# The sum across partitions in a spectral filter: two VectorE instructions, or two accumulating DMAs from GpSimd

## The chip, the cores and the metric

The kernel runs on one core of a Trainium2 chip. The metric is the device time of one execution in microseconds (us), as a median of several runs. The engines are TensorE (PE in the profile; its weight loads are PEld), VectorE (DVE), ScalarE (ACT), GpSimd (POOL) and SyncE (SP), which here only issues DMAs. Each has a queue of its own and takes its instructions in order. SBUF is the memory on the chip, with 128 partitions; matmuls write to PSUM. SP, ACT and GpSimd can issue DMAs.

## The reference

A spectral filter over the sequence, then a block with a low-rank mixing of the sequence and an MLP over the channels:

```python
# x: (8, 3136, 256); filt_r, filt_i: (1569, 256)
X = np.fft.rfft(x, axis=1)
Y = X * (filt_r + 1j * filt_i)[None]
y = np.fft.irfft(Y, n=3136, axis=1)

h = y.transpose(0, 2, 1) @ U @ V                 # U: (3136, 32), V: (32, 3136)
u = y + h.transpose(0, 2, 1)
out = u + np.maximum(u @ w_ch1, 0.0) @ w_ch2     # 256 -> 1024 -> 256
```

Inputs and outputs are float32; inside, the kernel works in float16 with sums in float32.

## The kernel before, in words

The 3136 points are split as 49 x 64, and both transforms are done by matmuls. For each of the 8 batches:

- `f1` (L206, evictions L211) transforms over the 49 points. Frequencies k1 = 1 to 24 with real and imaginary part, and k1 = 0, go to DRAM (`ct1`, `ct0`). For batches 0 and 1 `f1_turned` and `turn` (L231, L256) do the same without the way through DRAM.
- `mid` takes the frequencies in 13 pairs (`PAIRS`; k1 = 0 stands alone as the third). For each: a matmul over the 64 points (`pz`, L318; L320 for k1 = 0), with 64 real parts on partitions 0 to 63 and 64 imaginary parts on partitions 64 to 127; one VectorE product with the real and the imaginary part of the filter at once (L326), which leaves two products `uv[:, 0]` and `uv[:, 1]`; and stage 3 (`s3`: matmul `pe`, L287, eviction by ScalarE to `e3`, L296; L290 for k1 = 0). A tile `uv` holds two pairs (k1 = 0 has one of its own), three such tiles are in rotation, and `s3` runs three pairs behind.
- A complex product needs sums across the halves: the real half takes away the imaginary half's second product, the imaginary half adds the real one's. In batches 1 to 7 L330 and L331 do this on VectorE when a tile is complete, in place, so `s3` needs one matmul. In batch 0 it is left to PE: a second matmul with the weights `gsm`, which are `gm` with its halves swapped and a sign.
- `s3` stores its results to DRAM (`ct2`, L301), and `load_e2` (L343) reads them back into `eb` with k1 on partitions 32 to 79. The row of k1 = 0 goes the same way: one store (L291), and four loads `load_e20` into partition 80 (L346). `eb` has one buffer.
- `rank` (L353 to L364) makes the low-rank term in the frequency domain from `e3` and puts it into partitions 0 to 31 of `eb` with VectorE (L364). `s4` (L379, evictions L384, L386) transforms back over k1 into `ut`.
- The MLP runs in 49 groups of 512 points, each of 8 steps: `mm1` (L411) with ReLU on ScalarE (L414), and for the group before `mm2` (L434) with the residual (L426), an eviction by VectorE every fourth step (L441) and a store every eighth (L446).

`x` is loaded from GpSimd's queue (L110), as it is cast to float16 on the way; so are the filters (L137, L139), whose copies to partitions 64 to 127 `spread_filters` makes (L144, L145). Nearly all other DMAs are issued by SP.

The order: all that comes before `first.close()` (batch 0, and half of `f1` for batch 1) is issued as written. From there, the MLP's 392 steps are the backbone. A section is the 48 steps of one batch's MLP; `deal` spreads the next batch's `mid` over the section's steps 2 to 24 (8 to 31 in the first section), then its `eb` loads, `rank` and `s4`; `f1` of the batch after it is spread from step 18 (28 in the first) on, and the loads of `x` at steps 4, 9, 14 and 19. What is written in this way is a priority: a scheduler sets the order on each engine ahead of the run, and lets an instruction go ahead of its place when it reckons that its inputs are there. In the trace the loads of the k1 = 0 row are issued from 139.62 us on, before the last stores L301 of the same `mid`, which are written ahead of them.

Of the kernel before, what the change touches and what calls it, by code (L numbers as in the profile page):

```python
# [25 lines left out]
def _consts():  # L26
    f16 = np.float16
    q, r = np.arange(NQ), np.arange(NR)
    k2 = np.concatenate([np.arange(32), np.arange(63, 31, -1)])
    k1 = np.arange(1, NK)  # L30


    ws = np.zeros((98, 32, 98))
    for h in range(2):
        for j in range(32):
            w = np.exp(-2j * np.pi * np.outer(64 * q + 32 * h + j, k1) / SEQ)
            ws[h::2, j, 24 * h:24 * h + 24] = w.real
            ws[h::2, j, 48 + 24 * h:72 + 24 * h] = w.imag
            ws[h::2, j, 96 + h] = 0.5

    e = np.exp(-2j * np.pi * np.outer(r, k2) / NR) / 8
    a2 = np.block([[e.real, e.imag], [-e.imag, e.real]])
    a2[:, 96:] *= -1
    f = e.T
    g = np.block([[f.real, -f.imag], [f.imag, f.real]])
    g[96:] *= -1
    gs = np.roll(g, 64, axis=0)
    gs[64:] *= -1  # L50

    rows = [64 * c + 32 * h + j for j in range(32) for c in range(2) for h in range(2)]
    m64 = np.concatenate([a2[rows], g, gs, 2 * a2], axis=1)


    sv = np.zeros((49, NR, NQ))
    ph = 2 * np.pi * np.outer(k1, np.arange(SEQ)) / SEQ
    ph = ph.reshape(24, NQ, NR).transpose(0, 2, 1)
    sv[0:48:2] = 2 / 49 * np.cos(ph)
    sv[1:48:2] = -2 / 49 * np.sin(ph)  # L60
    sv[48] = 1 / 49

    kr = np.tile(np.eye(RANK), (4, 4))
    return (ws.reshape(98, 32 * 98).astype(f16), m64.astype(f16),
            sv.reshape(49, SEQ).astype(f16), kr.astype(f16))
# [3 lines left out]
def kernel(  # L69
# [19 lines left out]

    ct1 = [nc.dram_tensor(f"ct1_{b}", (32, 96, DM), F16, kind="Internal") for b in range(NB)]  # L90
    ct0 = [nc.dram_tensor(f"ct0_{b}", (NR, DM), F16, kind="Internal") for b in range(NB)]
    ct2 = [nc.dram_tensor(f"ct2_{b}", (49, NR, DM), F16, kind="Internal") for b in range(NB)]

    cst = ctx.enter_context(tc.tile_pool(name="cst", bufs=1))
    sb = ctx.enter_context(tc.tile_pool(name="sb", bufs=1))
# [46 lines left out]
    def spread_filters(i):  # L142
        s = slice(PARTS[i], PARTS[i + 1])
        nc.vector.tensor_copy(fab[64:128, 0, s, :], fab[0:64, 0, s, :])  # L144
        (nc.scalar.copy if i else nc.vector.tensor_copy)(fab[64:128, 1, s, :], fab[0:64, 1, s, :])  # L145

    for i in range(3):
        load_filters(i)
# [117 lines left out]
    def mid(b, tag="z"):  # L266
# [14 lines left out]
        def s3(ks, uv, o):  # L281
            n = len(ks) * DM
            i = (ks[0] - 1) // 2
            m = 128 if ks[0] else 64
            pe = ps.tile([128, 512], F32, tag=tag, bufs=2, name="pe")
            for f, w in enumerate((gm, gsm) if b == 0 else (gm,)):
                nc.tensor.matmul(pe[0:m, 0:n], w[:, 0:m], uv[:, f, o:o + n], start=(f == 0), stop=(b > 0 or f == 1))  # L287
            if not ks[0]:
                e3[b, 6] = sb.tile([64, DM], F16, tag="e30", bufs=2, name="e30")
                nc.scalar.copy(e3[b, 6], pe[0:64, 0:n])  # L290
                nc.sync.dma_start(dram(ct2[b], 48 * NR * DM, [[DM, 64], [1, DM]]), e3[b, 6])  # L291
                return
            if i % 2 == 0:
                e3[b, i // 2] = sb.tile([128, 4, DM], F16, tag="e3", bufs=7, name="e3")
            t = e3[b, i // 2]
            nc.scalar.copy(t[:, 2 * (i % 2):2 * (i % 2) + 2, :].rearrange("p k d -> p (k d)"), pe)  # L296
            if b == 0 and i > 9:
                nc.sync.dma_start(dram(ct2[b], 2 * i * 128 * DM, [[DM, 128], [128 * DM, 2], [1, DM]]),
                                  t[:, 2 * (i % 2):2 * (i % 2) + 2, :])
            elif i % 2:  # L300
                nc.sync.dma_start(dram(ct2[b], 2 * (i - 1) * 128 * DM, [[DM, 128], [128 * DM, 4], [1, DM]]), t)  # L301
# [6 lines left out]
        for i, ks in enumerate(PAIRS):  # L308
            n = len(ks) * DM
            if b == 0 and i in (2, 6):  # L310
                spread_filters(i // 4 + 1)
            if b < 2 and i in (3, 7):
                load_a2(i // 4 + 1)
            pz = ps.tile([128, 512], F32, tag="z", bufs=2, name="pz")
            if ks[0]:
                src = a2[(ks[0] - 1) // 8]
                k = (ks[0] - 1) % 8
                nc.tensor.matmul(pz, a2m, src[:, k:k + 2, :].rearrange("p k d -> p (k d)"), start=True, stop=True)  # L318
            else:
                nc.tensor.matmul(pz[:, 0:n], a20m, a2[3], start=True, stop=True)  # L320
            o = 512 if ks[0] % 4 == 3 else 0
            if o == 0:
                uv = sb.tile([128, 2, 1024], F16, tag="uv", bufs=3, name="uv")
            zin = bass.AP(tensor=pz.tensor, offset=pz.offset, ap=[[pz.ap[0][0], 128], [0, 2], [1, n]])
            fin = view(fab[:, 0, ks[0], 0:1], 0, [[NK * DM, 2], [1, n]])
            nc.vector.tensor_mul(uv[:, :, o:o + n], zin, fin)  # L326
            todo.append((ks, uv, o))
            if b and (o or not ks[0]):

                nc.vector.tensor_sub(uv[0:64, 0, 0:o + n], uv[0:64, 0, 0:o + n], uv[64:128, 1, 0:o + n])  # L330
                nc.vector.tensor_add(uv[64:128, 0, 0:o + n], uv[64:128, 0, 0:o + n], uv[0:64, 1, 0:o + n])  # L331
            if len(todo) > (3 if b else 2):
                s3(*todo.pop(0))
            yield
        for it in todo:
# [5 lines left out]

    def load_e2(b, g):
        nc.sync.dma_start(eb[32:80, 8 * g:8 * g + 8, :], dram(ct2[b], 8 * g * DM, [[NR * DM, 48], [1, 8 * DM]]))  # L343

    def load_e20(b, g, eng):
        eng.dma_start(eb[80:81, 16 * g:16 * g + 16, :],  # L346
                      dram(ct2[b], (48 * NR + 16 * g) * DM, [[NR * DM, 1], [1, 16 * DM]]))

    def rank(b):
        ph = ps.tile([128, 512], F32, tag="z", bufs=2, name="ph")  # L350
# [127 lines left out]
    next(ranks[0])  # L478
    for g in range(8):
        load_e2(0, g)  # L480
        if g % 2 == 0:
            load_e20(0, g // 2, nc.scalar)
    for _ in ranks[0]:
        pass

# [16 lines left out]

    def loads(b):
        for g in range(8):
            if g % 2 == 0:
                load_e20(b, g // 2, nc.sync)
            load_e2(b, g)
        yield

    for b in range(1, NB):  # L510
        a, z = S[b - 1], S[b]
        e = z - 17 if b == 1 else z - 24
        deal(mids[b], 17, a + {1: 8, 2: 5}.get(b, 2), e)
        plan[e + 2].append(loads(b))
        deal(ranks[b], 5, e + 3, e + 8)
        deal(s4s[b], 16, e + 8, z)
        if b == 1:
            deal(f1s[1], 4, 0, 6)
        if b + 1 < NB:
            for c in range(4):  # L520
                plan[a + (1 if b == 1 else 4) + (2 if b == 1 else 5) * c].append(later_x(b + 1, c))
            deal(f1s[b + 1], 8, a + (28 if b == 1 else 18), z - (6 if b == 1 else 13))
# [40 lines left out]
```

## Time and profile before

| | |
|---|---|
| median of 3 runs (lowest to highest) | 559.17 us (558.14 to 560.31) |
| the profiled execution | 556.45 us |
| its span, first to last instruction | 554.7 us |
| busy: PE, DVE, ACT, POOL | 519.0, 388.6, 344.3, 37.1 us |
| L326, 96 products of 128 x 1024 / 8 of 128 x 512 | 113.5 / 5.4 us, 1219 / 681 ns each |
| L330 and L331, 42 each of 64 x 1024 | 28.9 and 28.8 us, 687 and 685 ns each |
| L330 and L331, 7 each of 64 x 256 | 2.0 and 2.0 us, 288 and 285 ns each |
| L441, 98 evictions of the MLP | 66.6 us, 684 ns each |
| DMA packets, MB, mean rate | 86174, 88.43 MB, 159 GB/s |
| of these from GpSimd's queue | 7632 packets, 15.94 MB |
| SP issues of `eb` by L346 (k1 = 0) | 28 of 8 KB, median 317 ns each |

The times are of one profiled execution; it is shorter than the median of the runs by 2.7 us. "Busy" of PE is modelled, since matmuls overlap, so a high share does not say that PE runs at its peak; the number of matmuls in a stretch of time says more. A row of a group names the line, the engine, the operation and the tiles, with the number of instructions, their busy time, and the mean of one. The DMA share is a mean over the 16 DMA engines.

### The profile page before, as it was taken

To read this page: it belongs to the slowest core of one execution; us is meant where nothing else is said; L and a number is where in the kernel's file an instruction comes from. 1 tells how busy PE (TensorE), PEld (TensorE's weight loads), DVE (VectorE), ACT (ScalarE), POOL (GpSimd) and SP (SyncE) were. 2 spreads that over 40 slices of the span, in tenths; PEclk is the share of its full clock that TensorE was granted. 3 is DMA by queue.
4 is the path that set the end of the run, shared out by engine and by line. 5 is a ranking of instruction groups with operands and counts; after the bars stand their busy time and mean duration, and the time that the engine had idled before them with its cause. 6 is when DMAs were issued, how large, how long until landed. Compare 5 with 4: busy or idle time off the path is not lost.

```text
span 554.7 us, 11907 instructions
## 1 busy us (share of the span) xinstructions
PE 519.0 (94%) x4794; PEld 353.0 (64%) x4794; DVE 388.6 (70%) x542; ACT 344.3 (62%) x629; POOL 37.1 (7%) x61
## 2 busy tenths in 40 slices
PE   4766999999999899999999999999999999999997
PEld 4425656776667656676567856676667755676665
DVE  3975598777996399776997489775987489751111
ACT  3766777646775557645775557646675567656663
POOL 6541000100010000000010000000000000000000
PEclk9985899999999999999999999999999999999999
DMA  9997624983579635865499454874458334622113
GB/s 192 170 231 177 115 80 118 255 244 135 124 175 290 182 101 129 231 180 193 105 216 291 104 176 118 224 198 155 128 162 250 109 108 134 189 81 77 53 63 113
DMA packets 86174, 88.43 MB, mean 159 GB/s; under 512 B 5059, under 2 KB 76803, under 8 KB 86088
## 3 DMA queue, kind: packets, MB, share of 16 engines
q1 hardware_dynamic: 78480, 71.72, 41.7%
q0 software_dynamic: 7632, 15.94, 17.0%
q8 instruction: 37, 0.61, 0.4%
q14 instruction: 17, 0.14, 0.1%
q10 hardware_dynamic: 8, 0.03, 0.0%
HBM read 55.43 MB, written 48.17 MB: 187 GB/s over the span
## 4 chain that ended last, share of the span: by engine, by line
PE 65%; DVE 14%; DMA 8%; issue 4%; ACT 2%; SPq 1%; POOL 1%; ACTq 0%; POOLq 0%
PE phh L411 24%; PE pc L434 23%; DVE uv L326 7%; PE pu L379 5%; DMA eb<-ct 3%; PE pz L318 3%; PE pe L287 3%; PE pc L426 3%; DMA a<-ct 3%; PE pf L206 3%; DVE uv L330 2%; DVE uv L331 2%; DVE och L441 2%; ACT h L414 1%; POOL sv L170 1%
## 5 line engine op out<-in xcount | busy, mean ns | idle before, releaser
L414 ACT ACTIVATE h<-phh 128x512 f16<-128x512 f32 x392 | 232.6, 598 | 154.7 <-PE phh L411 149.7
L434 PE MATMUL pc<-w2sb,h 128*128 128x256 f16 x1568 | 246.0, 272 | 0.0
L411 PE MATMUL phh<-ut,w1sb 128*128 128x512 f16 (+7 forms) x896 | 241.3, 354 | 1.8 <-ACT h L414 1.2
L434 PEld LDWEIGHTS <-h 128*128 128x128 f16 x1568 | 148.7, 97 | 87.8 <-issue 8.0
L326 DVE TENSOR_TENSOR uv<-pz,fab 128x1024 f16<-128x1024 f32 (+1 forms) x104 | 118.3, 1177 | 11.9 <-PE pz L318 10.5
L441 DVE COPY och<-pc 128x512 f32<-128x512 f32 x98 | 66.6, 684 | 84.2 <-PE pc L426 84.1
L411 PEld LDWEIGHTS <-w1sb 128*128 128x128 f16 x896 | 76.6, 98 | 23.9 <-issue 10.1
L386 DVE CAST ut<-pu 128x392 f16<-128x392 f32 x120 | 65.0, 562 | 33.2 <-PE pu L379 26.9
L296 ACT CAST e<-pe 128x512 f16<-128x512 f32 x96 | 55.4, 587 | 14.3 <-PE pe L287 13.5
L426 PE MATMUL pc<-idn,ut 128*128 128x128 f16 (+1 forms) x400 | 55.3, 219 | 0.0
L379 PEld LDWEIGHTS <-eb 81*128 81x128 f16 x1024 | 42.0, 99 | 11.5 <-issue 3.4
L379 PE MATMUL pu<-sv,eb 81*128 81x49 f16 x1024 | 45.7, 189 | 3.0 <-DMA eb<-ct 2.9
L287 PE MATMUL pe<-uv,m 128*128 128x512 f16 (+1 forms) x117 | 41.4, 384 | 4.0 <-ACT e L296 1.5
L364 DVE COPY eb<-h 32x4096 f16<-32x4096 f16 x32 | 37.7, 1208 | 6.8 <-ACT h L361 6.7
L426 PEld LDWEIGHTS <-ut 128*128 128x128 f16 (+1 forms) x400 | 37.7, 98 | 7.1 <-issue 0.8
L318 PE MATMUL pz<-a,m 128*128 128x512 f16 x96 | 35.8, 385 | 5.8 <-DMA a<-ct 2.8
L110 POOL DMA_DIRECT2D x<-in_x_dram x36 | 20.9, 584 | 299.4 <-PE pf L206 194.8
L211 DVE CAST asb<-pf 98x512 f16<-98x512 f32 x48 | 32.5, 683 | 8.1 <-PE pf L206 7.9
L206 PE MATMUL pf<-x,ws 98*98 98x256 f16 x192 | 34.7, 273 | 0.4 <-ACT asb L211 0.2
L211 ACT CAST asb<-pf 98x512 f16<-98x512 f32 x48 | 28.3, 589 | 6.9 <-PE pf L206 6.5
L330 DVE TENSOR_TENSOR uv<-uv 64x1024 f16<-64x1024 f16 (+1 forms) x49 | 30.9, 630 | 1.3
L331 DVE TENSOR_TENSOR uv<-uv 64x1024 f16<-64x1024 f16 (+1 forms) x49 | 30.8, 628 | 0.9
(59 smaller groups left out, 183.3 us busy)
## 6 DMA issues: line engine op xcount, KB each, us to landing
out_dram<-och SPq DMA_DIRECT2D x48, 512.0 KB
eb<-ct SPq DMA_DIRECT2D x64, 192.0 KB
ct<-e SPq DMA_DIRECT2D x47, 256.0 KB
x<-in_x_dram POOLq DMA_DIRECT2D x28, 392.0 KB, 7.0
ct<-asb SPq DMA_DIRECT2D x24, 384.0 KB
a<-ct SPq DMA_DIRECT2D x18, 512.0 KB
x<-in_x_dram POOLq DMA_DIRECT2D x4, 384.0 KB, 7.9
ws<-ws SPq DMA_DIRECT2D x1, 600.2 KB
```

The lines of the kernel that those rows point to most:

```text
L211: (nc.vector.tensor_copy if i else nc.scalar.copy)(dst, src)
L287: nc.tensor.matmul(pe[0:m, 0:n], w[:, 0:m], uv[:, f, o:o + n], start=(f == 0), stop=(b > 0 or f == 1))
L296: nc.scalar.copy(t[:, 2 * (i % 2):2 * (i % 2) + 2, :].rearrange("p k d -> p (k d)"), pe)
L318: nc.tensor.matmul(pz, a2m, src[:, k:k + 2, :].rearrange("p k d -> p (k d)"), start=True, stop=True)
L326: nc.vector.tensor_mul(uv[:, :, o:o + n], zin, fin)
L379: last = nc.tensor.matmul(pu[:, NQ * i:NQ * i + NQ], eb[:, 8 * g + i, d], sv[:, 8 * g + i, :], start=(i == 0), stop=True, skip_group_check ...
L386: nc.vector.tensor_copy(dst, src)
L411: nc.tensor.matmul(ph[:, o:o + n], w1sb[:, dh, 128 * t:128 * t + 128], utv(b)[:, dh, t0:t0 + n], start=(dh == 0), stop=(dh == 1), skip_gro ...
L414: nc.scalar.activation(h, ph, RELU)
L426: nc.tensor.matmul(d, w, idn, start=False, stop=(dh == 1), skip_group_check=True)
L434: nc.tensor.matmul(o, gr.h[tt][:, 128 * i:128 * i + 128], w2sb[:, tt, :], start=(tt == 0), stop=False, skip_group_check=True)
L441: nc.vector.tensor_copy(gr.och[:, i - 1:i + 1, :], gr.pc.rearrange("p (j d) -> p j d", d=DM))
```

## The change

VectorE's subtraction and addition (L330, L331) go. In their place GpSimd issues two DMAs per tile `uv`, each of which adds 64 partitions of `uv[:, 1]` to the other 64 partitions of `uv[:, 0]` within SBUF. As these only add, the sign moves into the filter: the copy of its imaginary part on partitions 64 to 127 is made with a factor of -1, and `gs` loses its sign for batch 0. `s3` runs five pairs behind instead of three in batches 1 to 7, `uv` has four buffers instead of three, and `mid` is dealt in 19 pieces instead of 17. The row of k1 = 0 no longer goes through DRAM: one DMA from SP writes it from the 64 partitions of `e3[b, 6]` into partition 80 of `eb`; `load_e20` and the row 48 of `ct2` go.

```diff
-    gs[64:] *= -1
...
-    ct2 = [nc.dram_tensor(f"ct2_{b}", (49, NR, DM), F16, kind="Internal") for b in range(NB)]
+    ct2 = [nc.dram_tensor(f"ct2_{b}", (48, NR, DM), F16, kind="Internal") for b in range(NB)]
...
     def spread_filters(i):
         s = slice(PARTS[i], PARTS[i + 1])
         nc.vector.tensor_copy(fab[64:128, 0, s, :], fab[0:64, 0, s, :])
-        (nc.scalar.copy if i else nc.vector.tensor_copy)(fab[64:128, 1, s, :], fab[0:64, 1, s, :])
+        (nc.scalar.mul if i else nc.vector.tensor_scalar_mul)(fab[64:128, 1, s, :], fab[0:64, 1, s, :], -1.0)
...
                 nc.scalar.copy(e3[b, 6], pe[0:64, 0:n])
-                nc.sync.dma_start(dram(ct2[b], 48 * NR * DM, [[DM, 64], [1, DM]]), e3[b, 6])
+                nc.sync.dma_start(eb[80:81, :, :], e3[b, 6])
                 return
...
             if o == 0:
-                uv = sb.tile([128, 2, 1024], F16, tag="uv", bufs=3, name="uv")
+                uv = sb.tile([128, 2, 1024], F16, tag="uv", bufs=4, name="uv")
...
             if b and (o or not ks[0]):
-                nc.vector.tensor_sub(uv[0:64, 0, 0:o + n], uv[0:64, 0, 0:o + n], uv[64:128, 1, 0:o + n])
-                nc.vector.tensor_add(uv[64:128, 0, 0:o + n], uv[64:128, 0, 0:o + n], uv[0:64, 1, 0:o + n])
-            if len(todo) > (3 if b else 2):
+                for p in range(2):
+                    nc.gpsimd.dma_start(uv[64 * p:64 * p + 64, 0, 0:o + n], uv[64 - 64 * p:128 - 64 * p, 1, 0:o + n],
+                                        accum_op=mybir.AluOpType.add)
+            if len(todo) > (5 if b else 2):
                 s3(*todo.pop(0))
...
-    def load_e20(b, g, eng):
-        eng.dma_start(eb[80:81, 16 * g:16 * g + 16, :],
-                      dram(ct2[b], (48 * NR + 16 * g) * DM, [[NR * DM, 1], [1, 16 * DM]]))
...
     for g in range(8):
         load_e2(0, g)
-        if g % 2 == 0:
-            load_e20(0, g // 2, nc.scalar)
...
     def loads(b):
         for g in range(8):
-            if g % 2 == 0:
-                load_e20(b, g // 2, nc.sync)
             load_e2(b, g)
         yield
...
-        deal(mids[b], 17, a + {1: 8, 2: 5}.get(b, 2), e)
+        deal(mids[b], 19, a + {1: 8, 2: 5}.get(b, 2), e)
```

## The prediction

> **What bounds the kernel now.** I read the page's table of 40 slices first: TensorE (PE) stands at 9 tenths from slice 8 on, and VectorE (DVE) at 7 to 9 in bursts that come back every 64 us. PE "busy" is modelled, so I then asked for busy times in stretches cut at those bursts, where the counts of instructions tell more than the shares. A burst holds one batch's `mid` (its 13 multiplications with the filter); the stretch behind it holds that batch's `eb` loads, `rank` and `s4`.
>
> ```profile
> core 0: us, PE busy (x) PEld busy (x) DVE busy (x) ACT busy (x) POOL busy (x), PEclk, DMA share, GB/s
> 64.00:94.00 30.00, 29.25 (x210) 17.85 (x209) 28.68 (x36) 21.71 (x38) 0.00 (x0) 1.00 0.29 87
> 94.00:128.00 34.00, 33.76 (x390) 24.89 (x389) 21.63 (x34) 20.54 (x38) 2.61 (x4) 1.00 0.91 248
> 128.00:157.50 29.50, 29.05 (x207) 17.30 (x205) 28.15 (x36) 20.89 (x39) 1.11 (x2) 1.00 0.37 98
> ...
> 445.00:474.00 29.00, 28.54 (x191) 16.66 (x192) 26.87 (x33) 19.39 (x35) 0.00 (x0) 1.00 0.34 109
> ```
>
> In the bursts (rows 1, 3, 4) DVE is busy 28.15 of 29.5 us, PE gets through 207 matmuls; in the stretch between (row 2) 390 in 34 us, with DVE at 21.6 of 34. The DMA engines are lightly loaded in the bursts (0.29 to 0.37) and nearly full behind them (0.91). VectorE's timeline in one burst shows the cycle:
>
> ```profile
> 142.04 0.68 DVE L331 TENSOR_TENSOR uv<-uv 64x1024 f16<-64x1024 f16 x1
> 142.75 2.35 DVE L326 TENSOR_TENSOR uv<-pz,fab 128x1024 f16<-128x1024 f32 x2
> 145.03 0.68 DVE L211 CAST asb<-pf 98x512 f16<-98x512 f32 x1
> 145.74 0.69 DVE L330 TENSOR_TENSOR uv<-uv 64x1024 f16<-64x1024 f16 x1
> 146.44 0.68 DVE L331 TENSOR_TENSOR uv<-uv 64x1024 f16<-64x1024 f16 x1
> 147.15 2.35 DVE L326 TENSOR_TENSOR uv<-pz,fab 128x1024 f16<-128x1024 f32 x2
> ```
>
> Two products, one eviction, the exchange (L330, L331), without a gap: 4.4 us for two pairs of k1, of which the exchange is 1.4. Thus in the bursts DVE sets the pace.
>
> PE's need in a burst comes from the chain of waits (start, us, what), which holds only the part of each matmul that nothing overlaps:
>
> ```profile
> 203.48 0.43 PE phh L411 x2
> 203.91 0.22 PE pz L318
> 204.13 0.44 PE pc L434 x4
> ...
> 208.55 0.11 PE pc L426 x2
> ```
>
> Two L411 take 0.43 us, four L434 0.44 and one L426 0.055, together 0.925 for a step of the MLP; one L318 or L287 takes 0.22, and one L206 0.11. The burst 128 to 157.5 has 79 L434 (19.75 steps, 18.3 us), 12 + 13 of L318 and L287 (5.5), 18 of L206 (2.0): 25.8 us of 29.5. By the same counts the seven bursts (64 to 94, 128 to 157.5, 194 to 223, 257 to 285, 320 to 349, 385 to 413, 445 to 474; with 2 us of L256 in the first) need 27, 25.8, 26.2, 24.5, 25.5, 24.2 and 26.3, in all 179.5 us of 202.5. **The most that a free DVE can give is 23 us.** The stretches between need what they last (94 to 128: 27.5 steps 25.4, 28 of L206 3.1, `s4` 5.3, `rank` 1: 34.8 of 34) and give nothing.
>
> **The change part by part.**
>
> *Removed from DVE:* 42 + 42 exchanges of 0.69 us and 7 + 7 of 0.29 (L330 28.9 + 2.0, L331 28.8 + 2.0 us), 61.7 us, 8.8 per burst. DVE's need in a burst falls from about 28 to 19 us, below PE's 25.6 (179.5 / 7). So PE bounds the burst next: 28.9 becomes 25.6 at best.
>
> *Added on GpSimd:* 7 tiles per batch times 2 accumulating DMAs, 98 in all; 84 of 128 KB, 14 of 32 KB. Issue: the x loads show 0.55 us each, 7.7 us per batch on a queue that is busy 37.1 of 554.7 us. The descriptors queue with the x loads. What decides is the wait: stage 3 (L287) reads `uv` now after a DMA has landed. No row shows a transfer from SBUF to SBUF or one that adds. Nearest:
>
> ```profile
> q0 software_dynamic: 7632, 15.94, 17.0%
> ...
> x<-in_x_dram POOLq DMA_DIRECT2D x28, 392.0 KB, 7.0
> ...
> fab<-in_filt_r_dram POOLq DMA_DIRECT2D x2, 128.0 KB, 4.2
> ```
>
> GpSimd's packets take 0.170 x 554.7 x 16 / 7632 = 0.198 us. An x load has 98 rows of 4 KB in SBUF, some 196 packets, 12.25 per engine: 2.4 us. Its landing is 5.2 at least and 7.3 in the median over all loads of that line, so 2.8 to 4.9 is fixed. One accumulation has 64 rows of 2 KB, 4 packets per engine: 0.8 us, or 1.6 if the second read doubles it. So 3.6 to 6.5 us; I take 4.2, the row of the same 128 KB.
>
> The loop: from pz (0.38) by the product (1.22), the first issue (0.55), the second's landing (4.2), three handoffs and half an eviction ahead on DVE (together 0.65) L = 7.0 us. Stage 3 lies now 5 pairs behind, so between the pz that completes a tile and the first L287 on it there are 4 pairs; a burst has 13, thus 4 x 25.6 / 13 = 7.9 us at PE's pace. **7.0 fits in 7.9**, so the body costs nothing. Without that cover a burst lasts 13 x L / 4 = 3.25 L. At the end of a batch cover is thinner: the last product is dealt at step 15 of the section, its L287 at step 20, 5 steps of 0.925 and four L287, 5.5 us; 1.5 us late. PE's order is set ahead of the run and may put MLP matmuls in between, so I count half, 0.75 x 7 = 5 us. At most it is all, 10.5.
>
> *GpSimd's queue in front:* an accumulation waits in order for DVE; behind it stand later x loads, needed tens of us later by `f1`, so they cost nothing. The other way, an x load may stand ahead of an accumulation: 2.4 us of packets, and the wait for its buffer. The page has about one x load per burst (146.24, 216.76, 273.42, 342.77); with 0.9 us to spare 1.5 is left, half of the time: 0.75 x 7 = 5 us. From nothing, if x moves out of the bursts, to twice that.
>
> *A rule against the change:* the x issues take 0.55 us, but 0.95, 0.93 and 1.03 at 105.25, 160.39 and 286.87, each beside an `eb` copy (L364) on DVE. The Trainium skill says in "SBUF — State Buffer", on the two-port modes of DVE, that GpSimd can't write descriptors while such a copy runs; the trace agrees with 0.4 us more. In a burst there is no L364, so at 0.55 the sum stays; with 0.95 for both issues L is 7.8 and still fits.
> The Trainium skill gives in "DMA: Bandwidth & Descriptors", on the anatomy of one DMA, about 2.0 us plus bytes over 436 GB/s, an estimate of 2.3 us here; the sum would then be the full 23 us. The landings above (4.2 and 7.0) speak against so little, though they are from HBM.
>
> *The k1 = 0 row:* one SP DMA from `e30` in place of a store and four loads. 28 SP issues of 0.32 us go (L346), 1.3 us per batch in the bursts, where SP mostly waits for ACT (165 us). Its reader `s4` comes over 20 us after the copy, longer than an `eb` load takes (6.9 in the chain); cost nothing, gain up to the 5.1 us that PE waits for `eb`. I take 0. In batch 0 four ACT issues go (39.81 to 44.87, behind which ACT L237 and PE wait), but `s4` needs `eb` loads that SP issues from 41.98, and the x load that PE waits for at 54.2 is issued at 49.0 behind an `eb` group that lands at 48.5: gain 0 to 3.5, I take 0. The filter's sign in `spread_filters` is one operation for another of 0.48 to 2.75 us: 0, at most 0.5 more. The fourth `uv` buffer and the 19 steps add no instruction.
>
> Sum: -23 + 5 + 5 = **-13 us**. The profiled execution took 556.45 (span 554.7), so 543.4; the median of the three runs is 559.17, 2.7 higher, and the forecast on that scale is **546**.
>
> **Rivals.**
> *Slower: the landing becomes the pace.* If it exceeds about 5.6 us (L 8.4, burst 3.25 x 8.4 + half of (8.4 - 5.5) = 28.9, today's), PE waits at L287 longer than it waits for DVE today. At 6.2 (L 9.0): 29.3 + 1.8 = 31.0, +2.1 x 7 = 15, with the 5 for x +20: 579. For it: x loads land in 7.0, and an accumulation reads twice. Against: a third of the bytes, no HBM, idle DMA engines in the bursts.
> *No change:* landing 5.2 to 5.6, the wait for DVE replaced by an equal one for the DMA: about 558.
> *Full gain:* landing under 3.6, tail and x hidden: 536 to 539.
> *It does not run when it should:* GpSimd stands in front of x loads today (L110 waits 194.8 us for L206 in 12 waits). If one stands ahead of the accumulations 3 us too long per batch, -13 + 21 = +8: 567. For it: that wait; against: PE's order holds the same L206 ahead.
>
> **How the numbers follow.** Forecast 0.40, full gain 0.20, no change 0.13, landing as pace 0.22, GpSimd blocked 0.05. A measurement here tells about 0.5% (2.8 us) from no change: faster 0.60, same 0.13, slower 0.27. Range: low 530, the full 23 and the 5 to 6 us of `eb` waits and batch 0 together; high 580, the accumulation at 6.2.
>
> **What would show it.** L330 and L331 gone, DVE under 330 us; 98 more GpSimd issues of about 0.55; in a burst PE does the same counts in about 27 us; the landing of `uv` in the list of DMA issues near 4.2. Wrong if PE L287 or its weight load waits for a DMA on `uv` for more than some 15 us in total, if GpSimd's issues last over 1 us, or if the bursts are as long as before.

## The result: slower by 2.9%, and where the profile after shows it

The changed kernel takes 575.94 us (median of 4 runs, 571.88 to 576.93), the kernel before beside it 558.65: ratio 1.029, 95% interval 1.024 to 1.035. The forecast was 546. The profiled execution of the changed kernel took 571.88 us, its span is 570.1. L330, L287, L326 and L441 of before are now L330, L286, L325 and L437.

The page after, from its engines, queues, chain, groups and DMA issues (groups: busy us, mean ns | idle us ahead of them, and what ended most of it; issues: KB of one, median us to landing):

```profile
PE 514.7 (90%) x4794; PEld 353.0 (62%) x4794; DVE 329.9 (58%) x444; ACT 345.5 (61%) x629; POOL 120.1 (21%) x159
...
q0 software_dynamic: 15472, 27.41, 30.4%
...
PE 63%; DMA 14%; DVE 7%; issue 6%; POOL 3%; ACT 1%; SPq 0%; DVEq 0%; POOLq 0%; ACTq 0%
...
L330 POOL DMA_DIRECT2D uv<-uv x98 | 81.9, 1131 | 192.0 <-DVE uv L325 189.6
...
L286 PE MATMUL pe<-uv,m 128*128 128x512 f16 (+1 forms) x117 | 40.3, 372 | 29.1 <-DMA uv<-uv 24.0
...
uv<-uv POOLq DMA_DIRECT2D x84, 128.0 KB, 3.9
```

VectorE is relieved as announced (388.6 to 329.9 us busy), and stage 3 now waits for the accumulations. The list of waits (us in total, times, longest) has it for the matmul and, on an engine row of its own, for the weight load ahead of it:

```profile
PE pe L286 <- DMA uv<-uv: 24.0, 17, 3.4
...
PEld L286 <- DMA uv<-uv: 10.6, 7, 3.6
```

The two rows must not be added. They are mostly the same time, seen once by the weight load and once by the matmul behind it (an example stands below). What PE loses is the matmul's row, 24.0 us; the text goes by that row from here on.

Busy times from the first `pz` to the last `pe` of two bursts, before (the columns are those of the table in the prediction):

```profile
128.50:156.00 27.50, 27.05 (x179) 16.14 (x178) 26.56 (x33) 19.17 (x35) 0.55 (x1) 1.00 0.36 95
194.40:221.80 27.40, 26.79 (x174) 15.95 (x174) 26.52 (x32) 17.99 (x33) 0.56 (x1) 1.00 0.41 112
```

and of the same two after:

```profile
127.40:155.20 27.80, 23.08 (x151) 13.58 (x150) 19.28 (x20) 16.98 (x31) 12.31 (x15) 1.00 0.79 161
192.30:221.80 29.50, 23.39 (x152) 13.46 (x150) 19.30 (x20) 16.35 (x30) 12.31 (x15) 1.00 0.81 169
```

The bursts last as long as before (all seven: 27.8, 27.8, 29.5, 25.4, 26.1, 26.2 and 26.9 us; before 28.8 and six times about 27.5), but hold 28 and 22 matmuls fewer in these two. VectorE is no longer the pace (19.28 of 27.8), the DMA engines went from 0.36 to 0.79, and PE is idle for 4.7 and 6.1 us of them. The work that left the bursts, MLP steps, comes later: it did not become less.

One end of a burst, in the chain of work:

```profile
142.17 1.24 DVE uv L325
143.41 0.28 issue
143.69 0.43 POOL uv L330
...
146.80 0.58 POOL x L109
147.38 0.34 POOL uv L330
147.72 0.19 issue
147.91 7.26 DMA uv<-uv
155.17 0.04 issue
155.21 0.59 PE pe L286 x2
```

and in PE's timeline (start, us, what; in brackets the idle time ahead of it):

```profile
145.03 0.38 PE L317 MATMUL pz<-a,m 128*128 128x512 f16 x1
...
148.94 0.59 PE L286 MATMUL pe<-uv,m 128*128 128x512 f16 x2 [1.40 <-DMA uv<-uv]
...
152.85 0.27 PE L205 MATMUL pf<-x,ws 98*98 98x256 f16 x1
155.21 0.59 PE L286 MATMUL pe<-uv,m 128*128 128x512 f16 x2 [2.08 <-DMA uv<-uv]
...
214.51 0.59 PE L286 MATMUL pe<-uv,m 128*128 128x512 f16 x2 [1.84 <-DMA uv<-uv]
...
221.84 0.61 PE L286 MATMUL pe<-uv,m 128*128 128x512 f16 x2 [3.36 <-DMA uv<-uv]
```

The weight load ahead of the matmul at 155.21 waits in the same stretch:

```profile
154.40 0.10 PEld L286 LDWEIGHTS <-m 128*128 128x128 f16 x1 [1.53 <-DMA uv<-uv]
```

The last `pz` of the batch is at 145.03 and its L286 at 155.21. In these 10.2 us PE has 6.7 us of work and waits twice: 1.40 for the tile before, 2.08 for this one. The last two rows are the same two tiles one batch later. Of PE's 17 waits at L286, 13, with 20.5 of the 24.0 us, stand behind the last `pz` of their batch. The path: product, an x load ahead in GpSimd's queue (146.80, 0.58), two issues (from 147.38 on), a landing at 155.17.

### The profile page after: what moved, and what is told of

Same layout as the page of the kernel before. It is cut to its first block, busy times and chain, and to the rows that moved or that the text cites. A ratio compares the mean times of both kernels' runs of the same rounds, so it can differ in the third digit from the quotient of the medians.

```text
span 570.1 us, 12015 instructions
## 1 busy us (share of the span) xinstructions
PE 514.7 (90%) x4794; PEld 353.0 (62%) x4794; DVE 329.9 (58%) x444; ACT 345.5 (61%) x629; POOL 120.1 (21%) x159
## 4 chain that ended last, share of the span: by engine, by line
PE 63%; DMA 14%; DVE 7%; issue 6%; POOL 3%; ACT 1%; SPq 0%; DVEq 0%; POOLq 0%; ACTq 0%
PE phh L407 24%; PE pc L430 22%; DMA uv<-uv 10%; PE pu L375 4%; DVE uv L325 4%; PE pc L422 3%; PE pf L205 3%; PE pz L317 2%; PE pe L286 2%; DMA a<-ct 2%; POOL uv L330 2%; DVE eb L360 2%; DVE och L437 1%; POOL sv L169 1%; PE ph L349 1%
## 5 line engine op out<-in xcount | busy, mean ns | idle before, releaser
L325 DVE TENSOR_TENSOR uv<-pz,fab 128x1024 f16<-128x1024 f32 (+1 forms) x104 | 119.0, 1178 | 25.4 <-PE pz L317 24.5
L437 DVE COPY och<-pc 128x512 f32<-128x512 f32 x98 | 66.9, 686 | 102.5 <-PE pc L422 102.2
L330 POOL DMA_DIRECT2D uv<-uv x98 | 81.9, 1131 | 192.0 <-DVE uv L325 189.6
L286 PE MATMUL pe<-uv,m 128*128 128x512 f16 (+1 forms) x117 | 40.3, 372 | 29.1 <-DMA uv<-uv 24.0
L109 POOL DMA_DIRECT2D x<-in_x_dram x36 | 22.1, 617 | 138.1 <-PE pf L205 102.9
L375 PE MATMUL pu<-sv,eb 81*128 81x49 f16 x1024 | 46.7, 189 | 2.1 <-DVE eb L360 1.2
L375 PEld LDWEIGHTS <-eb 81*128 81x128 f16 x1024 | 42.7, 99 | 8.2 <-issue 1.9
L286 PEld LDWEIGHTS <-m 128*128 128x128 f16 (+1 forms) x117 | 10.7, 97 | 50.0 <-issue 34.5
L205 PE MATMUL pf<-x,ws 98*98 98x256 f16 x192 | 31.7, 273 | 0.1
```

What stands on the lines that cost most here:

```text
L330: nc.gpsimd.dma_start(uv[64 * p:64 * p + 64, 0, 0:o + n], uv[64 - 64 * p:128 - 64 * p, 1, 0:o + n], accum_op=mybir.AluOpType.add)
L375: last = nc.tensor.matmul(pu[:, NQ * i:NQ * i + NQ], eb[:, 8 * g + i, d], sv[:, 8 * g + i, :], start=(i == 0), stop=True, skip_group_check ...
L437: nc.vector.tensor_copy(gr.och[:, i - 1:i + 1, :], gr.pc.rearrange("p (j d) -> p j d", d=DM))
```

## The experiments

Each ratio is to the kernel before on the same chip (its medians there: 557.9 to 559.2 us). A letter or a theory in an expectation belongs to that run. The theory at the start: PE waits for the landing because too little work stands between a product and its stage 3. The rivals: the added DMAs disturb the other transfers; the direct row of k1 = 0 costs something; GpSimd's queue is blocked by x loads.

### The parts one by one

**The row alone**, in the kernel before:

```diff
-                nc.sync.dma_start(dram(ct2[b], 48 * NR * DM, [[DM, 64], [1, DM]]), e3[b, 6])
+                nc.sync.dma_start(eb[80:81, :, :], e3[b, 6])
...
-            if g % 2 == 0:
-                load_e20(b, g // 2, nc.sync)
```

> The kernel before with one part of the change alone: the k1 = 0 row by one DMA from e30. Both theories (PE waits for late accumulations at the end of each batch; the accumulations load the DMA engines) put nothing of the loss here: within 0.5% of before, 556 to 561 us. If it is over 565, the row's DMA carries a part of the loss.

568.5 us, ratio 1.019 (1.016 to 1.022): 10.5 us slower, where I had expected nothing. `s4` waits for `eb`; its line in the list of waits is

```profile
PE pu L375 <- DMA eb<-ct: 13.3, 7, 3.8
```

and in the list of SP's own queue, of what its `eb` loads wait for (before: `ct<-e` 3.8, `out` 1.4):

```profile
SPq L343 <- DMA ct<-e: 11.5, 4, 3.7
...
SPq L343 <- DMA out_dram<-och: 7.2, 4, 2.9
```

PE waits 13.3 us in total for `eb` (before: 2.9), and SP issues some of the `eb` loads later (in one batch from 358.05 on over 10.00 us; before from 352.24 over 6.09).

**The changed kernel with its exchange back on VectorE** (the row, five pairs behind and four buffers stay):

```diff
-                    nc.gpsimd.dma_start(uv[64 * p:64 * p + 64, 0, 0:o + n], uv[64 - 64 * p:128 - 64 * p, 1, 0:o + n],
-                                        accum_op=mybir.AluOpType.add)
+                    nc.vector.tensor_add(uv[64 * p:64 * p + 64, 0, 0:o + n], uv[64 * p:64 * p + 64, 0, 0:o + n],
+                                         uv[64 - 64 * p:128 - 64 * p, 1, 0:o + n])
```

> The changed kernel with the exchange put back on VectorE (two additions per tile); stage 3 five pairs behind, four uv buffers, 19 pieces, the row and the sign stay. Both theories: the loss is in the DMAs, so about the time of before, 554 to 562 us. If it stays at 570 or more, the longer distance of stage 3 costs the time.

**No exchange at all** (in the diff above, the minus lines alone):

> The changed kernel without any exchange (the sums across the halves in batches 1 to 7 are left out: neither VectorE nor a DMA does them). It measures the most that a free VectorE can give: the prediction's count of PE's need says 23 us below before, 533 to 540 us. If it is 550 or more, the bursts have another bound than VectorE.

**The same DMAs, for which nobody waits** (the two halves of `uv` exchanged, so that the sums land where stage 3 does not read):

```diff
-                    nc.gpsimd.dma_start(uv[64 * p:64 * p + 64, 0, 0:o + n], uv[64 - 64 * p:128 - 64 * p, 1, 0:o + n],
+                    nc.gpsimd.dma_start(uv[64 * p:64 * p + 64, 1, 0:o + n], uv[64 - 64 * p:128 - 64 * p, 0, 0:o + n],
```

> The changed kernel with the same 98 accumulating DMAs, but turned round: they add uv[:, 0] to uv[:, 1], which nobody reads, so stage 3 waits for VectorE's product only (its sums across the halves are left out). Theory 1, PE waits for the landing: the loss goes, 534 to 546 us. Theory 2, the DMAs' load on the 16 DMA engines and on GpSimd slows the other transfers: it stays at 565 to 575 us.

| kernel | us | ratio (interval) | step |
|---|---|---|---|
| before | 558.0 | | |
| exchange on VectorE, rest as changed | 565.76 | 1.014 (1.009 to 1.018) | +7.7 row, order, buffers |
| no exchange | 540.33 | 0.968 (0.965 to 0.972) | -25.4 VectorE freed |
| same DMAs, nobody waits | 552.09 | 0.988 (0.984 to 0.993) | +11.8 load of the DMAs |
| changed kernel | 575.94 | 1.029 (1.024 to 1.035) | +23.9 the wait for them |

The last three have nearly the same order on PE (in four of seven batches the last `pe` is one or two MLP steps later in the changed kernel), so the last two steps hold little else; the first two hold changes of order as well. The last row was measured in another session than the others; by the ratios its step is 22.9 us. The exchange on VectorE came out 4 us above the range expected of it, and the DMAs for which nobody waits came out between the two theories. A freed VectorE is worth 25.4 us against the same kernel with the exchange on it, and 17.7 us against the kernel before; the prediction had 23. Without an exchange a burst is PE's:

```profile
126.00:146.50 20.50, 20.41 (x134) 12.01 (x132) 17.71 (x18) 15.09 (x28) 0.56 (x1) 1.00 0.36 99
```

The load of 11.8 us I had left out: GpSimd's queue has 7840 packets more, and their share of the 16 DMA engines' time rose from 0.170 x 554.7 to 0.304 x 570.1 us, 161 ns per packet; an accumulation has 80 of them, so it takes 0.8 us of all 16 DMA engines, and 14 of them some 11 us of a burst. In the kernel where nobody waits for them, PE waits 7.4 us for `eb` at `s4` (L375): the last `ct` store of a batch is issued up to 4.2 us after the last `pe` (1.5 without DMAs), and the first `eb` load up to 13.8 us after it (8.5). Its bursts are as short as without DMAs. In the changed kernel PE waits 0.5 us for `eb`. So the split into 11.8 and 23.9 holds for this order of taking parts out; it does not say that 11.8 us of the changed kernel's time are waits of that kind.

### Cover against landing

**Three pairs behind instead of five, and seven instead of five** (the second with five `uv` buffers, for which `asb` gives up one):

```diff
-            if len(todo) > (5 if b else 2):
+            if len(todo) > (3 if b else 2):
...
-        deal(mids[b], 19, a + {1: 8, 2: 5}.get(b, 2), e)
+        deal(mids[b], 17, a + {1: 8, 2: 5}.get(b, 2), e)
```

> The changed kernel with stage 3 three pairs behind instead of five (and mid dealt in 17 pieces, as before). Theory A, a chain of about 7 us per tile from pz through product, two issues and landing to stage 3, longer than the PE work between: two pairs between instead of four, so a burst lasts 13 x 7 / 2 = 45 us instead of 27, 650 to 710 us in all. Theory B, the throughput of GpSimd's issues or of the DMA engines limits the burst: the distance does not matter, 572 to 590 us.

```diff
-            asb = sb.tile([98, 8, DM], F16, tag="asb", bufs=4, name="asb")
+            asb = sb.tile([98, 8, DM], F16, tag="asb", bufs=3, name="asb")
...
-                uv = sb.tile([128, 2, 1024], F16, tag="uv", bufs=4, name="uv")
+                uv = sb.tile([128, 2, 1024], F16, tag="uv", bufs=5, name="uv")
...
-            if len(todo) > (5 if b else 2):
+            if len(todo) > (7 if b else 2):
...
-        deal(mids[b], 19, a + {1: 8, 2: 5}.get(b, 2), e)
+        deal(mids[b], 21, a + {1: 8, 2: 5}.get(b, 2), e)
```

> The changed kernel with stage 3 seven pairs behind (five uv buffers; three asb buffers instead of four, to make room). Theory A: six pairs between hide 7 us, only the end of a batch still waits: 554 to 565 us. Theory B: as the change, 572 to 580 us.

Three behind: 597.21 us in two runs, ratio 1.070 (1.063 to 1.077); L286 waits 43.7 us, bursts last 32 to 36 us. Seven behind: 568.46, ratio 1.018 (1.014 to 1.023). So the lag does decide, and in the direction that the theory said; three behind cost less than expected, and seven behind gained less. PE's own list of instructions tells why. I summed, by the prediction's row costs, the PE work that stands in it between the `pz` that completes a tile and the tile's first L286:

| pairs behind | tiles 1 to 5 of a batch | last two tiles | L286 waits for tiles 1 to 5 / the last two |
|---|---|---|---|
| 3 | 4.7 to 5.8 (the second tile 6.2 to 6.7) | 4.7 to 6.6 | 31.1 / 12.6 us |
| 5, the changed kernel | 5.6 to 7.2 (8.8 in one tile) | 4.7 to 6.1 | 5.0 / 19.1 us |
| 7 | 7.0 to 9.9 (10.6 in one) | 4.8 to 7.0 (8.2 in one) | 0 / 18.4 us |

The path to be covered is 7 us: 0.38 for `pz`, 1.22 for the product, 0.83 for an issue, 3.9 for the landing, 0.65 for the handoffs. Seven behind covers it in the first five tiles and not in the last two, behind which the batch has no more products: in the timeline all ten of its matmul waits (18.4 us) stand behind a batch's last `pz`. Five behind is nearly enough for the first five tiles already, although their cover is below 7 us in most cases: with 3.0 to 5.8 us (the second DMA of a tile) many of them land sooner than the median. At the end of a batch both sides are worse: the last tile but one lands in 4.6 to 5.6 us, the last in 3.8 to 8.8. (Where an expectation below speaks of 29 us of waits for seven pairs behind, it adds the weight loads' row.)

**Only the last tile on VectorE**, and **x loads held behind the last accumulation of a batch**, both in the changed kernel:

```diff
...
-                for p in range(2):
...
+                if ks[0] >= 23:
+                    for p in range(2):
+                        nc.vector.tensor_add(uv[64 * p:64 * p + 64, 0, 0:o + n], uv[64 * p:64 * p + 64, 0, 0:o + n],
+                                             uv[64 - 64 * p:128 - 64 * p, 1, 0:o + n])
+                else:
+                    for p in range(2):
...
```

> The changed kernel with only the last tile of each batch (k1 = 21 to 24) exchanged by VectorE; the other six tiles stay with the DMAs. Run e4 put the cost of waiting at 24 us, the DMAs' load at 12. Theory A, the wait is at the end of a batch, where only some 4 MLP steps stand between the last product and its stage 3: most of the 24 us go, 553 to 560 us. Theory B, the wait is spread over all tiles, since the planner packs the 13 pairs into 12 MLP steps instead of 16: only a part goes, 565 to 572 us.

```diff
-        load_x(b, c)
+        with tc.issue_after(added[b - 2].ins) if b > 2 else ExitStack():
+            load_x(b, c)
...
-                plan[a + (1 if b == 1 else 4) + (2 if b == 1 else 5) * c].append(later_x(b + 1, c))
+                if b == 1:
+                    plan[a + 1 + 2 * c].append(later_x(b + 1, c))
+            if b + 2 < NB:
+                for c in range(4):
+                    plan[z - (16 if b == 1 else 23) + 5 * c].append(later_x(b + 2, c))
```

> The changed kernel with the x loads of the batch after next held behind the last accumulation of a batch on GpSimd's queue. In the trace of the changed kernel an x load stands ahead of the last pair of accumulations in two batches only (146.80 and 211.88 us), and their landing is 7.3 and 8.9 us there. If x loads are the main cause of late landings, 560 to 566 us; if they matter in these two batches alone, 568 to 574 us.

(In the second, `added[b]` is the last accumulation of a batch.) 566.76 us (ratio 1.019, 1.013 to 1.024) and 568.09 (1.018, 1.014 to 1.022): 9 and 8 us of the changed kernel's loss come back, 6 in each by the ratios, and 17.4 and 18.8 us of waits at L286 (L287 in the second) stay. With the last tile on VectorE the last but one still waits 11.0 us. With the x loads behind, the last tile's waits fall from 7.8 to 3.1 us, those of the last but one stay at 12.2 (without: 11.3). Neither the last tile alone nor the x loads alone are the cause. The last two tiles on VectorE at five pairs behind were not run.

### The row of k1 = 0

**e7: the changed kernel with the row's old way through DRAM** (`load_e20` and its calls are back as well):

```diff
-                nc.sync.dma_start(eb[80:81, :, :], e3[b, 6])
+                nc.sync.dma_start(dram(ct2[b], 48 * NR * DM, [[DM, 64], [1, DM]]), e3[b, 6])
```

> The changed kernel with the k1 = 0 row back on its way through DRAM; exchange by DMA as changed. Run e1 showed that the row's part alone costs 10.5 us. If the parts add up: 563 to 568 us. If the row's part costs time only through the order that the planner makes of it, the two do not add up and the time is 570 us or more.

**e8: the kernel before with the direct DMA, and as many short DMAs on SP as before** (`load_e20` reads 64 elements into a tile that nothing uses):

```diff
+                nc.sync.dma_start(eb[80:81, :, :], e3[b, 6])
                 nc.sync.dma_start(dram(ct2[b], 48 * NR * DM, [[DM, 64], [1, DM]]), e3[b, 6])
...
-        eng.dma_start(eb[80:81, 16 * g:16 * g + 16, :],
-                      dram(ct2[b], (48 * NR + 16 * g) * DM, [[NR * DM, 1], [1, 16 * DM]]))
+        eng.dma_start(pad[:, g, :], dram(ct2[b], (48 * NR + 16 * g) * DM, [[NR * DM, 1], [1, 64]]))
```

> The kernel before with the direct DMA of the k1 = 0 row added, and the old store kept, and four small loads from it into a tile that nobody reads (so all DMAs of the old way stay in SP's queue, the loads shorter). If the direct DMA into one partition is itself what costs 10 us in e1: 566 to 570 us. If the loss comes from the order in which SP issues the eb loads, and from what they wait for, once the five DMAs of the old way are gone: 556 to 562 us.

**e12: e1 with the `eb` loads ahead of the next batch's stores:**

```diff
+                  with tc.issue_after(loaded[b - 1].ins) if c else ExitStack():
...
-        plan[e + 2].append(loads(b))
+        plan[e - 1].append(loads(b))
```

> As e1_row_only (kernel before, row of k1 = 0 by one direct DMA, old exchange), but SP issues the eb loads ahead of the next batch's asb stores that may stand in front of them. If the 10.5 us of the row alone come from eb loads that stand on SP behind slow stores, the waits of L375 and L379 for eb fall from some 18 to 3 to 8 us and the time is 557 to 562. If they come from the changed order of the other engines, or from the direct DMA, it stays at 565 to 570.

**e13: the kernel before with one DMA of 64 bytes more per batch:**

```diff
+                nc.sync.dma_start(pad, e3[b, 6][0:1, 0:32])
```

> The kernel before with one more SP DMA of 64 bytes per batch, from e30 to a tile that nothing reads, behind the store of the k1 = 0 row. By the rows of L346 it costs 0.3 us of SP's queue per batch: 557 to 560 if SP's order is robust. If the time hangs on which earlier DMA each SP DMA waits for (it moves by one in each batch), it is slower by 3 to 10 us: 562 to 569, with SP's waits of L343 grown and PE's order as before.

| kernel | us, ratio (interval) | PE waits for `eb` at `s4` | MLP steps from last `pe` to first `s4`, by batch |
|---|---|---|---|
| before | 558.6 | 2.9 us | 10, 10, 8, 9, 8, 10, 7 |
| e13, one tiny DMA more | 557.73, 0.998 (0.996 to 1.000) | 3.7 | the same |
| e8, direct row, dummies | 564.34, 1.012 (1.008 to 1.016) | 7.0 | 11, 9, 7, 7, 9, 6, 7 |
| e1, direct row | 568.5, 1.019 (1.016 to 1.022) | 13.3 | 10, 9, 8, 8, 9, 9, 6 |
| e12, `eb` loads first | 574.71, 1.030 (1.027 to 1.033) | 18.1 | 10, 6, 5, 6, 5, 6, 6 |
| changed kernel | 575.94, 1.029 (1.024 to 1.035) | 0.5 | 11, 13, 14, 11, 14, 14, 10 |
| e7, changed, old row | 580.06, 1.040 (1.034 to 1.047) | 5.4 | 11, 11, 7, 9, 10, 8, 8 |

e13 moves SP's queue by one DMA in each batch and costs nothing: that rival falls. e8, with the direct DMA and dummies in place of the old ones, came out between its two ranges. e12 was to bring the 10 us back and lost 6 more: the order put `s4` 5 or 6 steps behind the last `pe` in six batches, and it stands there and waits. Its line:

```profile
PE pu L377 <- DMA eb<-ct: 18.1, 4, 5.2
```

In the kernels with VectorE's exchange at three pairs the time follows the wait for `eb` (the first five rows of the table: 10.4 us more of it in e1, and 10.5 us more time). In the changed kernel, with 10 to 14 steps between, the direct row costs nothing, and undoing it lost 4 us more. So the row's price is no fixed cost of its DMA: it goes with where the order puts `s4` and the `eb` loads, which an edit of this size moves. What in the row's edit makes SP's `eb` loads late in e1, whose distances are almost those of before, I did not separate further.

### Is there a version that beats both?

**No DMA, every second tile's sum by PE's second matmul (`gsm`, as in batch 0), the others on VectorE; and the same with the old row:**

```diff
+    def by_pe(ks):
+        return (ks[0] - 1) // 4 in (1, 3, 5)
...
-            for f, w in enumerate((gm, gsm) if b == 0 else (gm,)):
+            both = b == 0 or by_pe(ks)
+            for f, w in enumerate((gm, gsm) if both else (gm,)):
```

> No DMA for the exchange: in batches 1 to 7 three tiles of seven (k1 = 5 to 8, 13 to 16, 21 to 24) are summed by PE with a second matmul on the swapped weights, as batch 0 is, and the other four by VectorE; the rest as changed. VectorE needs a burst of 19 + 5 = 24 us at most, PE 3 x 2 x 0.22 = 1.3 us more per batch. From run e3 (540.3 us without exchange): 540 + 9 = 549, range 545 to 556 us. If it is over 557, a burst that is balanced between PE and VectorE has no gain.

> e11_mixed_pe (no DMA adds; every second tile's sum on PE by a second matmul) with the old way of the k1 = 0 row through DRAM. If the parts add, the row's 8 to 10 us come back: 545 to 548. If the row's price is one of the order that happens to come out, as e7 against the changed kernel says: 552 to 560.

554.43 us, ratio 0.993 (0.990 to 0.996), and with the old row 575.04, ratio 1.030 (1.027 to 1.033). The row's 8 to 10 us do not add: here the direct row gains 20.6. Again `s4` moved, from 8 to 15 steps behind the last `pe` to 7 to 11, and PE's waits for `eb` from 1.9 to 8.7 us; that accounts for a third of it, the rest I have not traced. With the old row the time is above both ranges that were expected.

**Seven pairs behind, the last two tiles on VectorE, x loads behind the last accumulation** (e14), and three kernels that each put one of these back: all tiles on VectorE (e16), all on DMAs (e17), x loads at their old places (e18). Buffers and pieces are as in the run with seven pairs, `added` and the places of the x loads as in the run that holds them back:

```diff
...
-            if len(todo) > (5 if b else 2):
+            if len(todo) > (7 if b else 2):
...
+                if ks[0] >= 19:
+                    for p in range(2):
+                        nc.vector.tensor_add(uv[64 * p:64 * p + 64, 0, 0:o + n], uv[64 * p:64 * p + 64, 0, 0:o + n],
+                                             uv[64 - 64 * p:128 - 64 * p, 1, 0:o + n])
...
+        with tc.issue_after(added[b - 2].ins) if b > 2 else ExitStack():
+            load_x(b, c)
```

> The best DMA version that the waits point to: seven pairs behind, the last two tiles (k1 = 17 to 24, added from k1 = 19 on) on DVE, x loads behind the last accumulation. Theory A (what is lost is cover in the tail and the DMA load): the 29 us of waits of e10_lag7 on its last two tiles go, 7/10 of the DMA load stays, DVE takes back 2 of 7 tiles (some 7 of 25 us): 551 to 560, about the kernel before. Rival (accumulating DMAs disturb stores and eb loads whatever the cover): 563 to 568.

> e14_lag7_tail_x with all seven tiles of a batch added on DVE and no accumulating DMA; seven pairs behind, five uv buffers, three asb buffers and the x loads behind stay. If e14 is fast because five of seven exchanges have left DVE, this is slower than e14 by about 5/7 of the 25.4 us that the whole exchange was worth: 557 to 567. If it is fast because of the order that the longer way and the moved x loads bring, this stays at 540 to 548.

> e14_lag7_tail_x with the last two tiles of a batch on accumulating DMAs again. If the end of the batch is where the cover is too short (29 us of waits on those tiles in e10_lag7), the waits of L286 for uv come back there: 555 to 568. If e14 owes its time to the x loads alone, 540 to 548.

> e14_lag7_tail_x with the x loads at their old places, in front of accumulations of the next batch in part. If x in front of the accumulations or beside them on the DMA engines costs what the step (e) of the prediction had, 5 to 10 us: 547 to 553. If it costs what e6 gave to the changed kernel, 8 us: 550. If the loads do not matter once the cover is long: 541 to 545.

| kernel | us | ratio (interval) |
|---|---|---|
| e14: five tiles by DMA, last two on VectorE, x behind | 542.57 | 0.973 (0.970 to 0.975) |
| e18: x at its old places | 546.06 | 0.977 (0.974 to 0.980) |
| e17: all seven tiles by DMA | 565.69 | 1.014 (1.009 to 1.018) |
| e16: all seven tiles on VectorE | 579.51 | 1.037 (1.034 to 1.040) |

**e14 beats both kernels, by 16 us the kernel before**, and is 8 us below the range that was expected. The controls say why. The last two tiles on DMAs cost some 23 us (e17 against e14; likewise 22.4 for e10 against e18, which differ in that alone), the x loads 2 to 4 (546.06 against 542.57; by the ratios 2.4), and five of seven exchanges on VectorE 36.9, more than the 18 that 5/7 of 25.4 gave: e16's bursts are VectorE's again (27.8 us in five batches, 28.8 and 30.8 in the others, against 21.5 to 22.4 and, in the first, 26.5 in e14; 40 us in all). e16 is also 20 us slower than the kernel before, which has the same exchange on VectorE, so not all of the 36.9 is the price of the exchange: the longer way and its order cost there, too. e17's list of waits has

```profile
PE pe L287 <- DMA uv<-uv: 16.3, 9, 3.5
```

all of it behind the last `pz` of a batch. That is not yet the 23 us. For the same matmuls PE is busy 517.6 us in e17 and 512.4 in e14, as its clock was lower in places; the rows of the granted clock in 40 slices, e17 and then e14, are

```profile
PEclk9996899999999998999999997999999999999999
...
PEclk9995899999999999999999999999999999999999
```

In e17 the granted clock is 0.50 for 3.4 us from 216.3 and from 281.1, and for 6.8 us from 346.0. Each of these stretches begins in a wait at L287 or 0.2 us behind it (2.5 us up to 216.38, 2.8 up to 280.89, 3.5 up to 347.24). e14 has no wait of PE above 2 us after its first 60 us, and its clock is 1.00 from 62 to 539. So a long wait cost more here than its own length. The four runs of the changed kernel follow the clock as well: 571.88 us at a mean granted clock of 0.985, 576.93 at 0.973.

e14's list of waits has no wait of stage 3 for a DMA, and none of `s4` for `eb`: its order puts `s4` 11 to 17 steps behind the last `pe`. From e14's page, and its busy times in two of the bursts:

```profile
PE 512.4 (95%) x4794; PEld 355.0 (66%) x4794; DVE 346.5 (64%) x472; ACT 340.5 (63%) x629; POOL 97.2 (18%) x131
...
PE 84%; issue 4%; ACT 2%; DVE 2%; DMA 2%; POOL 1%; ACTq 0%; DVEq 0%; POOLq 0%
...
uv<-uv POOLq DMA_DIRECT2D x56, 128.0 KB, 3.7
```

```profile
127.60:149.50 21.90, 21.49 (x141) 12.90 (x139) 20.63 (x23) 15.21 (x29) 8.96 (x11) 1.00 0.71 146
190.00:212.20 22.20, 22.13 (x144) 12.93 (x142) 20.43 (x22) 14.54 (x28) 9.53 (x12) 1.00 0.86 202
```

PE is busy in the whole burst, VectorE nearly so, and the chain that ended last is 84% PE's (changed kernel: 63%). The DMA engines are as full as in the changed kernel (0.71 and 0.86); it does not matter here, since no matmul waits for an accumulation. e14 is some 2 us above the kernel without any exchange.

## Why the prediction was wrong, point by point

- *The bursts are VectorE's, and a free VectorE gives at most 23 us*: right in size. Without the exchange 25.4 us against the same kernel with it, 17.7 against the kernel before.
- *What goes and what comes*: VectorE lost 58.7 us of busy time of the 61.7 reckoned (its other groups, each up to 0.7 us longer, took back most of the rest). An accumulation of 128 KB landed after 3.9 us in the median (taken: 4.2), its 0.8 us of packets were right, and the issue was 0.83 us where two follow each other, mean 1.13 (taken: 0.55). With these the path L comes to the predicted 7.0.
- *7.0 fits in 7.9, so the body costs nothing*: the 7.9 was wrong, but it cost little. It spread 25.6 us of PE work evenly over the 13 pairs. A part of a burst's work stands behind the last `pz`, though: by the same row costs PE has 20 to 21 us of work from the first `pz` to the last in the kernel before, and 15 in the changed kernel (18 in its first batch). The cover is 6.1 us in the mean of a batch's first six tiles. The change itself, which deals the batch in 19 pieces over the same 22 steps, gives this ahead of any run: 22/19 is 1.16 steps for a pair, so four pairs are 4.3 us of steps and, with four `pz` and four L287, 6.0 us. That VectorE is free does not do it alone: with three pairs behind and 17 pieces VectorE is as free, and the stretch holds 19 to 21 us. With 19 pieces and the exchange on VectorE it holds 17 to 21. Since many of the first tiles land early, only 5.0 us of waits fall on the first five tiles of all seven batches.
- ***The end of a batch, half of 1.5 us times 7*: the step that failed.** The term was put at 5 us, and at most at 10.5. PE waits 20.5 us behind the batches' last `pz`, and 19.1 us for the last two tiles (11.3 for the last but one, 7.8 for the last); with the 5 us for x loads, which fall on the same waits, the forecast had half of that. The prediction counted one late tile in a batch where two are late, took half, and took 4.2 us for a landing that is 4.6 to 5.6 us for the last tile but one and 3.8 to 8.8 for the last. The cover it had reckoned, 5.5 us, was about right: 4.7 to 6.1. In the version with seven pairs, moving these two tiles to VectorE gains some 23 us (e17 against e14): 16.3 of waits at L287, and 5.2 of longer busy time of PE at a lower granted clock. Why the last accumulations land late is shown in part: holding back the x loads shortens the two longest landings (7.3 and 8.8 us to 5.2 and 6.9), and the others stay.
- *An x load ahead, 5 us*: the size was right, 2 to 4 us in e18 against e14, 6 to 8 in the changed kernel.
- *The load on the DMA engines*: missing from the sum, 11.8 us in e4. The Trainium skill says in "DMA: Bandwidth & Descriptors", on issuing engines, that DMAs of all engines interleave on the same 16 DMA engines whoever issued them; e4's late `ct` stores on SP's queue agree. The load is no fixed price: in e14, with 70 of 98 DMAs and `s4` later in the order, hardly any of it is left.
- *The row, nothing*: right in the changed kernel (0.5 us of waits for `eb`), though alone it cost 10.5. The 5.1 us that PE was said to wait for `eb` before the change add the weight load's row to the matmul's, 2.9. Row, order and buffers together were put at nothing; with the exchange back on VectorE they cost 7.7 us, which I have not taken apart.
- *The page's 2.0 us plus bytes over 436 GB/s*: the Trainium skill's formula ("DMA: Bandwidth & Descriptors", on the anatomy of one DMA) gives an estimate of 2.3 us; the shortest landing of 128 KB here was 2.7, the median 3.9, the longest 8.9. The measurement decides.
- *The rival "the landing becomes the pace"* came closest (579 us, from a landing of 6.2 for every tile). Its price was right by luck: the landing did not set the pace of the bursts' bodies, it came late at their ends; the load of the DMAs, and the 7.7 us of row, order and buffers, which the rival did not have, made up the rest. All three signs that were given for a wrong forecast came: L286 waits 24.0 us for a DMA on `uv` (bound: 15), the issues last over 1 us in the mean, and the bursts are as long as before.

## What to carry to other kernels

Cover for a new latency must be counted in the order that the changed kernel will have, not in the old one: more pieces dealt over the same steps set the pairs closer together, and a distance of four pairs buys less time than it did. Look at the end of each batch first, where no following work of the same kind hides anything, and count every tile that ends there; keep the short synchronous way for these and give the long way, at a longer distance, to the tiles in the middle, which here turned +17 us into -16. And where an order is fixed ahead by a planner, a single part that is put in or taken out moves other instructions too: compare the waits and the order, not times alone, before a difference is put down to the part. And before two rows of a list of waits are added, look in the timeline whether they are the same time.

## What the hardware showed that I had not expected

An accumulating DMA from SBUF to SBUF (64 rows of 2 KB) takes 0.81 to 1.78 us per issue on GpSimd (mean 1.13, two in a row 1.66 together; a plain load of x takes 0.55) and lands 2.7 to 8.9 us later (median 3.6 with the 14 of 32 KB), the two longest with an x load ahead of them in the queue. A wait of PE of 2.5 to 3.5 us was followed by a stretch at half the granted clock in three cases of e17 (3.4, 3.4 and 6.8 us). And the same change of the k1 = 0 row moved the time by +10.5 us in the kernel before, by -4 in the changed kernel (e7 without it is slower) and by -20.6 in e11: a fixed cost of the transfer cannot do that; it goes with the order that follows from the edit.
